# An attention and feed-forward kernel on one core: the second batch in split fp32r units in place of whole float32 pairs of heads

## The chip, the cores and the metric

The kernel runs on one core of a Trainium2 chip. The metric is the device time of one execution in microseconds. Unless a number is said to be of the profiled execution, times are medians of several executions. TensorE is called PE in the profile, its weight load PEld, VectorE is DVE, ScalarE is ACT, GpSimd is POOL, SyncE is SP.

## What is computed

Eight batches of eight heads, 576 positions and 64 dimensions go through attention with a sliding window of 128 positions and a linear bias per head; its output, 4608 tokens of 512 numbers, goes through a feed-forward layer with 2048 hidden units.

```
scores = scale * np.matmul(q, k.transpose(0, 1, 3, 2))
bias = slopes[:, None, None] * (-np.abs(rel).astype(np.float32))[None, :, :]
mask = (rel >= 0) & (rel < window)
scores = np.where(mask, scores + bias[None], -1000000000.0)
scores = scores - np.max(scores, axis=-1, keepdims=True)
attn = np.exp(scores)
attn = attn / (np.sum(attn, axis=-1, keepdims=True) + 1e-09)
attn_out = np.matmul(attn, v)
...
x = attn_out.transpose(0, 2, 1, 3).reshape(B * S, H * D)
h = x @ w_in
g = h * (1.0 / (1.0 + np.exp(-1.702 * h)))
out = g @ w_out
```

## The kernel before

**The feed-forward layer.** The tokens are cut into 18 chunks of 256, the hidden units into 16 groups of 128. One step is one chunk and one group: `up` makes h with twelve 128x256 matmuls (L552), ACT takes the tanh (L557), DVE makes g (L558), ACT casts it to fp32r as gh (L561), POOL makes the remainder gl = g - gh (L562), and `down` adds six 128x512 matmuls to the chunk's accumulators (L571): four with gh, two with gl. g, gh, gl and h have two buffers each. There are 288 steps. They go by chunk, but chunk 0 is done in two halves around chunk 1: steps 0 to 7 are chunk 0, steps 8 to 23 chunk 1, steps 24 to 31 the rest of chunk 0, and each later chunk has 16 steps. `split_x` makes high and low parts of a chunk of x (L536 on DVE or ACT, L538 on DVE and POOL).

**The weights** come as 64-bit words and are decoded once, in 32 halves: ACT L211, DVE L212 and L213, ACT L216, POOL L217. Three halves are decoded ahead of the steps and the rest in the first 22 or so steps.

**The attention of a batch** is made in one of two forms, chosen by the batch's number: below `WB` the whole form, from `WB` on the split form.

- *Whole form* (`part_batch`, `WholeUnit`): a unit is a pair of heads and a part of the positions (0 to 256, 256 to 512, 512 to 576), so 12 units to a batch. Everything stays float32. Scores are float32 matmuls of 64 rows of each head (L324, two records to a matmul in the trace), DVE adds the bias and takes the minimum (L351), ACT takes the exponential (L374), DVE the reciprocal (L392, L393). The normalization is done on POOL (L402) and ACT (L399) in turn, the transposes on PE (L419), ACT copies them out (L427), PE multiplies with v (L476), ACT copies the result to x (L485).
- *Split form* (`whole_batch`, `Unit`): both heads of a pair are laid end to end, 9 blocks of 128 positions, worked on by two (the last unit has one), so 5 units to a pair and 20 to a batch. Every operand is split in two fp32r numbers. ACT casts Q (L292) and V (L299), DVE casts K (L310), POOL makes the remainders of Q (L311), K (L312) and V (L300). Scores are two fp32r matmuls to a block (L334), then DVE L362, ACT L381, DVE L392 and L393, the normalization on DVE (L406), transposes (L442), ACT's cast of the transposed weights (L455), DVE's remainder (L461), the products with V (L499), and a sum of both halves: ACT L520, POOL L523, DVE L526 and L529. POOL clears parts of a block (L361, L367).

**What sets the order.** One `tick` moves all units in flight by one stage. The loop over the steps issues ticks at a pace that has each batch's units done before the chunk that reads them begins; the list `due` holds how many units are wanted and by which chunk. A unit of batch b may start when chunk `start` has begun. In the whole form each part of a batch has an entry of its own, by the chunk of its first position; in the split form the batch has one entry, by the chunk of its first position. A scheduler then moves instructions within each engine's queue, and each engine runs its queue in order. SP issues the loads, in program order; the loads of a unit are issued one tick after another, between the fetches of weights.

```
for b in range(B):
    start = max((b * S + S - 1) // T - XBUFS, 0)
    if b < WB:
        for lo, hi in ((0, 2 * P), (2 * P, 4 * P), (4 * P, S)):
            units += part_batch(b, lo, hi)
            due.append((len(units), (b * S + lo) // T, start))
    else:
        units += whole_batch(b)
        due.append((len(units), b * S // T, start))
```

Of the kernel before, what the change touches and what calls it, by code (L numbers as in the profile page):

```python
# [33 lines left out]
FAR = 1.0e37  # L34
DEPTH = 3
BESIDE = range(4)
WB = 2
DECODE_TICKS = 5, 6, 7
FETCH_AHEAD = 6
PINNED = 8  # L40
# [102 lines left out]
def tile_kernel(ctx: ExitStack, tc: tile.TileContext, q0, k0, v0, qT, kT, v, w_in, w_out, out):  # L143
# [9 lines left out]
    def move(dst, src):  # L153

        tc.keep_in_program_order(nc.sync.dma_start(dst, src))
# [78 lines left out]
    def load(u):  # L234
# [8 lines left out]
        u.rk = raw.tile([P, 3 * P], F32, name="rk", tag="rk")  # L243
        move(u.rq[:, :u.nq], qT[u.pair - WB * NP, :, u.q0:u.q0 + u.nq])
        move(u.rk[:, :u.nk], kT[u.pair - WB * NP, :, u.k0:u.k0 + u.nk])

# [24 lines left out]
    def load_v(u):  # L271
# [8 lines left out]
        if full:  # L280
            move(u.rv[:, :full], v[u.pair - WB * NP, at:at + full * P, :].rearrange("(c p) d -> p c d", p=P))
            u.spans.append((P, slice(0, full)))
        if full < len(u.loaded):
            m = u.loaded[-1].n
            move(u.rv[:m, full], v[u.pair - WB * NP, at + full * P:at + full * P + m, :])
            u.spans.append((m, slice(full, full + 1)))
# [306 lines left out]
# [4 lines that stand above are left out]
# [135 lines left out]
def lay_out(q, k, v, moe_w_in, moe_w_out):  # L732
    import numpy as np

    def pairs(a):

        n = len(a) * NP
        return np.asarray(a).reshape(n, 2, S, D).transpose(0, 1, 3, 2).reshape(n, P, S)
# [7 lines left out]
    def words(w):  # L746
# [5 lines left out]
    lay = {  # L752
        "q0": pairs(q[:WB]),
        "k0": pairs(k[:WB]),
# [19 lines left out]
```

## Time and profile before

| | us |
|---|---|
| median of 3 runs | 1064.5 |
| lowest and highest | 1063.76, 1065.91 |
| the profiled execution | 1068.36 |
| its span, from the first to the last instruction | 1066.3 |
| mean granted PE clock in the span | 0.995 of full speed |

The profile is of one execution. A line of a view names the kernel's line, the engine, the operation, what it writes and reads, the shapes and the count; then come the busy time in us and the mean ns of one, and the engine's idle time before it with what ended most of it. A line of a window gives its length and the busy time and count of instructions of PE, PEld, DVE, ACT and POOL, then the granted PE clock, the mean share in which the DMA engines were busy, and GB/s. A line of the timeline starts with the start and the duration in us. In the chain of work that ended last, each share is of the window asked for.

### The profile page before, as it was taken

The page shows a single profiled execution, that of the slowest core. Times are in us where ns is not written, and L with a number is a line of the kernel's source. Part 1 is how long each engine was busy: PE and PEld are TensorE (multiplying, and loading weights), DVE is VectorE, ACT ScalarE, POOL GpSimd, SP SyncE. Part 2 cuts the span into 40 slices and gives each one's busy share as a digit, 9 for nine tenths or more (in the row PEclk, how much of TensorE's full clock was granted, in tenths as well). Part 3 has the DMA queues.
Part 4 walks back from the last instruction along what each step waited for, and adds up shares of the span by engine and source line. Part 5 has one row for each costly group of instructions (what it writes and reads, how often), then busy time and mean ns, then how long its engine had stood idle before and what let it go on. Part 6 is the DMA issues. An engine that isn't in the chain of part 4 may idle for free.

```text
span 1066.3 us, 21362 instructions
## 1 busy us (share of the span) xinstructions
PE 1052.9 (99%) x7041; PEld 929.1 (87%) x7041; DVE 660.5 (62%) x2117; ACT 597.2 (56%) x1811; POOL 603.5 (57%) x863
## 2 busy tenths in 40 slices
PE   9899999999999999999999999999999999999998
PEld 5567787889989999999999999999999999998987
DVE  6797522568887777545767668767877687313121
ACT  6879853466666565535555556655665656322222
POOL 4579933567676666554656557656666665323232
PEclk9899999999999999999999999999999999999999
DMA  8872001223222132102121223212222221000000
GB/s 307 281 261 73 25 22 56 73 67 96 75 76 81 51 102 67 57 14 71 54 79 52 71 62 91 66 60 78 79 63 85 57 78 28 20 2 20 1 21 20
DMA packets 88109, 78.45 MB, mean 74 GB/s; under 512 B 36800, under 2 KB 79296, under 8 KB 88000
## 3 DMA queue, kind: packets, MB, share of 16 engines
q1 hardware_dynamic: 82240, 67.14, 21.4%
q10 hardware_dynamic: 5760, 9.96, 2.6%
q8 instruction: 55, 0.90, 0.3%
q14 instruction: 54, 0.44, 0.1%
HBM read 67.63 MB, written 9.44 MB: 72 GB/s over the span
## 4 chain that ended last, share of the span: by engine, by line
PE 94%; DVE 3%; ACT 1%; DMA 1%; issue 1%; POOL 0%; SPq 0%; DVEq 0%; POOLq 0%; ACTq 0%
PE h_ps L552 38%; PE acc L571 37%; PE s_ps L334 5%; PE x_ps L499 5%; PE t_ps L442 4%; PE x_ps L476 2%; PE t_ps L419 1%; PE sb_ps L324 1%; PE s_ps L324 1%; DVE wc L213 1%; DMA rw<-w_out 1%; ACT pb L374 1%; DVE rec L392 0%; PE acc L189 0%; DVE rw L212 0%
## 5 line engine op out<-in xcount | busy, mean ns | idle before, releaser
L562 POOL TENSOR_TENSOR gl<-g,gh 128x256 fp32r<-128x256 f32 x288 | 218.0, 757 | 292.2 <-ACT gh L561 224.9
L552 PE MATMUL h_ps<-xh,w 128*128 128x256 f32 x2304 | 370.2, 284 | 1.1 <-POOL w L217 0.6
L552 PEld LDWEIGHTS h_ps<-xh,w 128*128 128x128 f32 x2304 | 328.5, 189 | 34.5 <-issue 2.8
L571 PE MATMUL acc<-w,gh 128*128 128x512 f32 x1152 | 324.9, 400 | 0.0
L558 DVE SCALAR_TENSOR_TENSOR g<-g,h_ps 128x256 f32<-128x256 f32 x288 | 119.6, 415 | 207.9 <-ACT g L557 206.5
L557 ACT ACTIVATE g<-h_ps 128x256 f32<-128x256 f32 x288 | 110.4, 383 | 229.4 <-PE h_ps L552 207.3
L571 PEld LDWEIGHTS acc<-w,gh 128*128 128x128 f32 x1152 | 196.5, 189 | 27.9 <-ACT g L557 0.3
L552 PE MATMUL h_ps<-xl,w 128*128 128x256 f32 x1152 | 194.6, 280 | 0.0
L561 ACT CAST gh<-g 128x256 fp32r<-128x256 f32 x288 | 116.9, 406 | 129.5 <-DVE g L558 121.1
L571 PE MATMUL acc<-w,gl 128*128 128x512 f32 x576 | 188.0, 401 | 0.0
L552 PEld LDWEIGHTS h_ps<-xl,w 128*128 128x128 f32 x1152 | 164.2, 188 | 6.0
L312 POOL TENSOR_TENSOR K<-rk,K 128x384 fp32r<-128x384 f32 (+1 forms) x120 | 109.0, 909 | 65.2 <-ACT Q L292 15.9
L381 ACT ACTIVATE pb<-pb,mins 128x256 f32<-128x256 f32 (+2 forms) x216 | 104.9, 487 | 43.8 <-DVE mins L362 40.1
L571 PEld LDWEIGHTS acc<-w,gl 128*128 128x128 f32 x576 | 92.6, 188 | 9.5 <-issue 0.9
L311 POOL TENSOR_TENSOR Q<-rq,Q 64x256 fp32r<-64x256 f32 (+1 forms) x120 | 83.1, 692 | 22.2 <-DVE K L310 4.9
L406 DVE TENSOR_SCALAR pb<-pb,rec 128x256 f32<-128x256 f32 (+2 forms) x216 | 91.8, 461 | 3.2
L362 DVE CUSTOM_DVE_ANT_0 pb<-s_ps,bias 128x256 f32<-128x256 f32 (+3 forms) x240 | 85.7, 377 | 4.1 <-PE s_ps L334 2.8
L392 DVE TENSOR_SCALAR rec<-sums 128x2 f32<-128x2 f32 (+3 forms) x144 | 48.5, 336 | 58.4 <-ACT pb L381 53.6
L334 PE MATMUL s_ps<-K,Q 128*128 128x256 f32 (+1 forms) x432 | 79.8, 289 | 0.4 <-DVE mins L362 0.4
L310 DVE CAST K<-rk 128x384 fp32r<-128x384 f32 (+1 forms) x120 | 52.5, 438 | 41.2 <-PE s_ps L334 34.2
L461 DVE TENSOR_TENSOR pl<-t_ps,ph 128x512 fp32r<-128x512 f32 (+2 forms) x120 | 72.2, 604 | 9.3 <-ACT ph L455 6.6
L442 PE MATMUL t_ps<-ident,pb 128*128 128x128 f32 x408 | 74.2, 272 | 0.0
(68 smaller groups left out, 1322.2 us busy)
## 6 DMA issues: line engine op xcount, KB each, us to landing
rk<-kT SPq DMA_DIRECT2D x72, 192.0 KB, 2.5
rq<-qT SPq DMA_DIRECT2D x96, 128.0 KB, 2.3
out<-o ACTq DMA_DIRECT2D x36, 256.0 KB, 2.1
rw<-w_in SPq DMA_DIRECT2D x16, 512.0 KB, 6.5
rw<-w_out SPq DMA_DIRECT2D x16, 512.0 KB, 7.0
rk<-kT SPq DMA_DIRECT2D x48, 128.0 KB, 2.2
rv<-v SPq DMA_DIRECT2D x96, 64.0 KB, 1.9
rq<-q SPq DMA_DIRECT2D x16, 128.0 KB, 2.6
```

The lines of the kernel that those rows point to most:

```text
L312: nc.gpsimd.tensor_tensor(K2, rk, K1.bitcast(F32), ALU.subtract)
L334: nc.tensor.matmul(u.s[:b.rows, e, b.first:b.end], u.Q[:, b.q0 - u.q0:b.q0 - u.q0 + b.rows], k[:, ko:ko + b.end - b.first], start=(z == 0) ...
L362: nc.vector.tensor_tensor_reduce(b.p[ra:rb, cs:b.end], u.s[ra:rb, e, cs:b.end], bias[head][ra:rb, cs:b.end], -SCALE, BIG, ALU.add, ALU.min ...
L381: nc.scalar.activation(live, live, AF.Exp, bias=u.mins[:b.rows, e:e + 1], scale=-1.0, accum_out=u.sums[:b.rows, e:e + 1],)
L406: nc.vector.tensor_scalar(live, live, u.rec[:rows, e:e + 1], None, ALU.mult)
L442: nc.tensor.transpose(u.t[:c.n, w:w + b.rows], b.p[:b.rows, col:col + c.n], ident[:b.rows, :b.rows])
L552: nc.tensor.matmul(h, w1[f][:, z, k * P:(k + 1) * P], x[:, k], start=(n == 0), stop=(n == len(ops) - 1))
L557: nc.scalar.activation(g, h, AF.Tanh, scale=0.851)
L558: nc.vector.scalar_tensor_tensor(g, g, 1.0, h, ALU.add, ALU.mult)
L561: nc.scalar.copy(gh, g)
L562: nc.gpsimd.tensor_tensor(gl, g, gh.bitcast(F32), ALU.subtract)
L571: nc.tensor.matmul(acc, g[:, t * P:(t + 1) * P], w2[f][:, z], start=(f == self.f0 and n == 0), stop=(f == self.f1 - 1 and n == 2))
```

## The change

`WB` becomes 1. Batch 1 is then worked on in 20 split units in place of 12 whole ones. Batch 0 stays whole, batches 2 to 7 stay split. The arrays handed to the kernel are cut at the same place (`lay_out` uses `WB`).

```
-WB = 2
+WB = 1
```

In `due`, batch 1 had three entries, four units each, wanted by chunks 2, 3 and 4; now it has one, 20 units, wanted by chunk 2, that is by step 32. So the pace of units is higher up to step 32 and lower from there on.

On POOL, near the end of chunk 1, the order of before has these rows. The rows with gl are the 17th to 20th, the 21st to 23rd and the 24th to 26th; pb is a whole unit's weights, x_306 and xh are chunk 0's x for its second half.

```order
L562 TENSOR_TENSOR gl<-g,gh 128x256 x4
L402 TENSOR_SCALAR pb<-pb,rec 128x256 x2
L562 TENSOR_TENSOR gl<-g,gh 128x256 x3
L402 TENSOR_SCALAR pb<-pb,rec 64x192
L538 TENSOR_TENSOR xl<-x_306,xh 128x256 x2
L562 TENSOR_TENSOR gl<-g,gh 128x256 x3
```

In the changed kernel POOL has these rows ahead of the 22nd and 23rd gl, behind the 21st; K, Q and VV are the operands of split units of batch 1, xb and carry their sums, and w_15 the last two halves of weights.

```order
L312 TENSOR_TENSOR K_2294<-rk,K_2293 128x256
L311 TENSOR_TENSOR Q<-rq,Q 64x256
L300 TENSOR_TENSOR VV<-rv,VV 128x2x64
L523 TENSOR_TENSOR xb<-xb,carry 64x128
L300 TENSOR_TENSOR VV<-rv,VV 128x2x64
L311 TENSOR_TENSOR Q<-rq,Q 64x256
L312 TENSOR_TENSOR K_2369<-rk,K_2368 128x384
L217 TENSOR_TENSOR w_15_2189<-wc,w_15_2189 128x512
L217 TENSOR_TENSOR w_15_2271<-wc,w_15_2271 128x512
L300 TENSOR_TENSOR VV<-rv,VV 128x2x64
L312 TENSOR_TENSOR K_2440<-rk,K_2439 128x384
L562 TENSOR_TENSOR gl<-g,gh 128x256 x2
```

Nothing stood between the 21st and the 22nd gl before; now eleven operations do, and the last weights are decoded behind the 21st gl instead of ahead of the 17th.

On PE, the down products of the last but one step of chunk 1 (weights w_14) stood like this before, t_ps being a whole unit's transposes and acc_1195 and acc_1196 the chunk's accumulators:

```order
L571 MATMUL acc_1195<-w_14_1649,gh 128x512
L571 MATMUL acc_1196<-w_14_1649,gh 128x512
L419 MATMUL t_ps<-ident,pb 128x128
L571 MATMUL acc_1195<-w_14_1649,gl 128x512
L571 MATMUL acc_1196<-w_14_1649,gl 128x512
L419 MATMUL t_ps<-ident,pb 128x128 x5
L552 MATMUL h_ps<-xh,w_8_1013 128x256
```

and now like this, with the transposes and scores of a split unit behind them:

```order
L571 MATMUL acc_1347<-w_14_2106,gh 128x512
L571 MATMUL acc_1348<-w_14_2106,gh 128x512
L552 MATMUL h_ps<-xh,w_8_1013 128x256 x6
L571 MATMUL acc_1347<-w_14_2106,gl 128x512
L571 MATMUL acc_1348<-w_14_2106,gl 128x512
L442 MATMUL t_ps<-ident,pb 128x128 x2
L334 MATMUL s_ps<-K_2439,Q 128x256
```

The up products of two steps further on (w_8) have moved ahead of the products with gl, and split matmuls stand where whole ones stood.

## The prediction

> **What bounds the kernel now.** I read the page first, then stretches of the first 160 us, then the chain of work that ended last, each time asking which engine is last.
>
> ```profile
> PE 1052.9 (99%) x7041; PEld 929.1 (87%) x7041; DVE 660.5 (62%) x2117; ACT 597.2 (56%) x1811; POOL 603.5 (57%) x863
> by line: PE h_ps L552 37.7%; PE acc L571 37.3%; PE s_ps L334 4.7%; PE x_ps L499 4.6%; PE t_ps L442 4.2%; PE x_ps L476 2.0%; PE t_ps L419 1.2%; PE sb_ps L324 1.2%; PE s_ps L324 1.0%; DVE wc L213 0.8%; DMA rw<-w_out 0.7%; ACT pb L374 0.5%; is
> ```
>
> By the averages TensorE (PE) is the bound and every other engine has 40% to spare. So a change is worth what it takes off PE, wherever PE is last. But averages hide stages; these are three stretches (columns: us, then busy time of PE, PEld, DVE, ACT, POOL):
>
> ```profile
> 53.50:95.70 42.20, 39.27 (x253) 28.39 (x251) 38.37 (x86) 36.48 (x115) 35.25 (x33) 0.96 0.55 185
> 95.70:125.50 29.80, 29.80 (x190) 23.08 (x190) 17.19 (x55) 29.25 (x87) 27.24 (x25) 1.00 0.18 49
> 125.50:158.30 32.80, 32.80 (x200) 25.56 (x198) 10.61 (x30) 17.92 (x52) 17.10 (x20) 1.00 0.09 24
> ```
>
> Up to 125 us, while weights are still decoded, POOL is busy 84% and 91%, ACT 86% and 98%. Only from 125 us has everything but PE room. The change works in exactly these stretches.
>
> **What it saves on PE.** The chain's line above prices attention on PE: the split form (L334, L499, L442) holds 4.7 + 4.6 + 4.2 = 13.5% of 1066.3 us for six batches, so 24.0 us a batch, 0.113 us for each of 1,272 rows. The whole form is best read where PE alone is last, from the end of the 24th step's down products on:
>
> ```profile
> 161.24 0.63 PE L571 MATMUL acc<-w,gl 128*128 128x512 f32 x2
> by line: PE h_ps L552 41.1%; PE acc L571 37.9%; PE x_ps L476 10.8%; PE t_ps L419 3.4%; PE s_ps L334 2.7%; PE sb_ps L324 2.5%; PE s_ps L324 1.7%; PE t_ps L442 0.7%
> 1000.24 1.40 PE h_ps L552 x12
> ```
>
> The second row is the chain from 161.9 to 218 us: the last whole rows (L476, L419, L324) hold 18.4% of 56.1 us = 10.3 us. By the order, 28, 16 and 5 of them stand behind the 144th down product, the end of the 24th step. In the changed kernel none does; instead 2 more L334, 11 more L442 and 18 more L499 stand there, 31 x 0.113 = 3.5 us, and 22 fewer up products (1.40 / 12 = 0.117 us each, 2.6 us), which PE has done earlier. **PE's work behind the 24th step shrinks by 10.3 - 3.5 + 2.6 = 9.4 us.** Batch 2 is also no longer hurried beside the rest of batch 1. The DVE waits on the chain near 307 us may go with that: between 0 and 3.5 us, of which I take 1.1 (PE itself was hardly idle there). Together 10.5 us.
>
> **What it costs ahead of the 24th step.** POOL's rows by shape (mean ns behind the busy time):
>
> ```profile
> L562 POOL TENSOR_TENSOR gl<-g,gh 128x256 fp32r<-128x256 f32 x288 | 218.0, 757 | 292.2 <-ACT gh L561 224.9 <-issue 15.3 <-PE acc L571 14.6
> L312 POOL TENSOR_TENSOR K<-rk,K 128x384 fp32r<-128x384 f32 x72 | 73.4, 1020 | 42.8 <-ACT Q L292 8.9 <-PE x_ps L499 8.3 <-DVE K L310 6.0
> L311 POOL TENSOR_TENSOR Q<-rq,Q 64x256 fp32r<-64x256 f32 x96 | 71.5, 745 | 17.7 <-DVE g L558 4.5 <-DVE K L310 2.4 <-ACT Q L292 1.7
> L300 POOL TENSOR_TENSOR VV<-rv,VV 128x128 fp32r<-128x128 f32 x96 | 46.6, 486 | 10.7 <-ACT VV L299 7.1 <-DVE K L310 1.7 <-POOL Q L311 0.5
> L217 POOL TENSOR_TENSOR w<-wc,w 128x512 fp32r<-128x512 f32 x32 | 45.9, 1442 | 6.6 <-ACT w L216 6.4
> L312 POOL TENSOR_TENSOR K<-rk,K 128x256 fp32r<-128x256 f32 x48 | 35.6, 742 | 22.4 <-ACT Q L292 7.0 <-ACT g L557 3.6 <-PE s_ps L334 3.3
> L402 POOL TENSOR_SCALAR pb<-pb,rec 128x256 f32<-128x256 f32 x20 | 19.4, 980 | 13.0 <-DVE rec L393 9.5 <-ACT w L216 3.5
> L523 POOL TENSOR_TENSOR xb<-xb,carry 64x128 f32<-64x128 f32 x48 | 22.3, 465 | 8.9 <-ACT xb L520 7.6 <-PE s_ps L334 0.5
> L311 POOL TENSOR_TENSOR Q<-rq,Q 64x128 fp32r<-64x128 f32 x24 | 11.6, 482 | 4.5 <-DVE K L310 2.5 <-DVE pb L406 0.4
> L402 POOL TENSOR_SCALAR pb<-pb,rec 128x128 f32<-128x128 f32 x12 | 9.8, 821 | 11.4 <-DVE rec L393 11.4
> L300 POOL TENSOR_TENSOR VV<-rv,VV 128x64 fp32r<-128x64 f32 x24 | 8.4, 350 | 4.2 <-ACT VV L299 3.1
> L402 POOL TENSOR_SCALAR pb<-pb,rec 64x192 f32<-64x192 f32 x8 | 7.2, 895 | 1.6 <-DVE rec L393 1.6
> L538 POOL TENSOR_TENSOR xl<-xf,xh 128x256 fp32r<-128x256 f32 x34 | 28.1, 841 | 5.7 <-PE h_ps L552 3.2 <-DVE xh L536 1.7 <-PE acc L571 0.5
> L361 POOL MEMSET pb<- 64x192 f32 x24 | 6.9, 286 | 7.3 <-PE t_ps L442 4.6 <-PE t_ps L419 1.8
> L367 POOL MEMSET pb<- 128x64 f32 x24 | 3.7, 154 | 2.5 <-PE t_ps L442 2.4
> ```
>
> Count what stands in POOL's order between the 2nd gl (L562) and the 24th, both kernels; the orders part only behind the 3rd. Common to both: 22 gl, 27 weight halves (L217), 4 remainders of x (L538), 38.9, 16.7 and 3.4 us, and 4 normalizations of 64x192. Gone: 17 normalizations (L402), 12 x 0.980 + 4 x 0.821 + 0.895 = 15.9 us. New: K2, 12 x 1.020 + 8 x 0.742 = 18.2; Q, 16 x 0.745 + 4 x 0.482 = 13.8; VV, 13 x 0.486 + 3 x 0.350 = 7.4; five carry adds 2.3; four memsets of each kind 1.8. That is 43.5 us, **net +27.6 us: 78.4 us of POOL work become 106.0 us**, in a stretch that lasts 104.8 us, from the 2nd gl's end to the 24th's:
>
> ```profile
> 52.80 0.72 POOL L562 TENSOR_TENSOR gl<-g,gh 128x256 fp32r<-128x256 f32 x1
> 124.80 0.75 POOL L562 TENSOR_TENSOR gl<-g,gh 128x256 fp32r<-128x256 f32 x1
> 157.59 0.73 POOL L562 TENSOR_TENSOR gl<-g,gh 128x256 fp32r<-128x256 f32 x1 [1.13 <-ACT gh L561]
> ```
>
> (158.3 - 53.5.) PE's down product needs gl, at most two steps later (g, gh and gl have two buffers), so POOL's queue now paces PE. At which rate does POOL get through such a queue? Up to 95.7 us, the 8th gl, the order of before holds 13 L217, 6 gl, 10 L402 and 2 L538, 34.0 us of mean durations in 42.2 us, a rate r of 0.80; from there to the 15th gl (124.80 + 0.75, second row) 11 L217, 7 gl and 6 L402, 26.9 us in 29.8, r = 0.90; both 0.845. What is lost is idle time (waits for ACT and DVE) and operations longer than their mean. A reason for the second stands in the trace:
>
> ```profile
> 242.43 0.17 DVE L392 TENSOR_SCALAR rec<-sums 128x2 f32<-128x2 f32 x1 [0.79 <-ACT pb L381]
> 247.05 0.73 POOL L311 TENSOR_TENSOR Q<-rq,Q 64x256 fp32r<-64x256 f32 x1
> 247.18 0.63 DVE L392 TENSOR_SCALAR rec<-sums 128x2 f32<-128x2 f32 x1 [0.82 <-ACT pb L381]
> L406 DVE TENSOR_SCALAR pb<-pb,rec x216: 279/354/1626, 199.1 to 906.5; 128x256 f32<-128x256 f32 x84, 128x128 f32<-128x128 f32 x12, 128x192 f32<-128x192 f32 x12
> ```
>
> The same DVE instruction takes 0.17 us, or 0.63 when a POOL operation runs: it ends 0.03 us behind POOL's end (247.78). L406, SBUF to SBUF like it, spreads from 279 to 1626 ns about a median of 354 (last row). I take it that L310, a third of that kind, and L406 meet the same, and that POOL waits in turn for one that has started. Ahead of the 24th g the change adds 19 L310, 29 L406 and 7 L392 to DVE, so r will hardly rise above what it was. The Trainium skill says, in "SBUF — State Buffer", section "SBUF: two separate sides", that DVE in such modes and GpSimd share one pair of ports as an exclusive lock held for the whole instruction; the rows agree that one waits, but only 0.03 of the waiter's 0.17 us was left when POOL ended, so less than a whole instruction is exclusive.
>
> I take r = 0.845 up to the 15th gl, where 67.3 us of work now stand (79.6 us), and 0.90 behind it, where decoding thins out, for 38.7 us (43.0): **122.6 us instead of 104.8, +17.8** (r = 0.864 overall). Nothing less than 106.0 us (r = 1) is possible; r = 0.80 gives 132.5.
>
> One thing comes back. Where POOL is last PE follows its gl closely, where PE is last it lags:
>
> ```profile
> 83.26 1.18 POOL L562 TENSOR_TENSOR gl<-g,gh 128x256 fp32r<-128x256 f32 x1
> 84.74 0.64 PE L571 MATMUL acc<-w,gl 128*128 128x512 f32 x2
> ```
>
> 85.38 - 84.44 = 0.9 us here, against 161.87 - 158.32 = 3.6 us at the 24th: 2.5 us less.
>
> **Sum:** span change = 106.0 / r - 104.8 - 2.5 - 10.5 = 106.0 / r - 117.8. With 0.864 it is **+4.8 us**; I round to +4.5. The profiled execution would be 1068.4 + 4.5 = 1072.9 us (span 1066.3 + 4.5, and 2.1 around it); it lies 3.9 us above the runs' median of 1064.5, so the **forecast for the median is 1069.0 us**. The whole saving on PE is larger than 10.5 us, but what falls ahead of the 24th step is spent waiting for POOL.
>
> Costed at nothing, by these rows (busy us over six batches; then over two):
>
> ```profile
> L455 ACT CAST ph<-t_ps 128x512 fp32r<-128x512 f32 (+2 forms) x120 | 62.2, 519 | 5.3 <-PE t_ps L442 3.8 <-PE x_ps L499 0.7
> L292 ACT CAST Q<-rq 128x256 fp32r<-128x256 f32 (+1 forms) x120 | 46.2, 385 | 16.9 <-PE s_ps L334 12.7 <-DMA rq<-qT 1.9 <-DVE pb L406 0.6
> L520 ACT COPY xb<-x_ps 64x512 f32<-64x512 f32 (+1 forms) x72 | 39.5, 549 | 3.5 <-PE x_ps L499 1.8
> L299 ACT CAST VV<-rv 128x128 fp32r<-128x128 f32 (+1 forms) x120 | 34.3, 286 | 3.9 <-PE x_ps L499 2.2 <-DMA rv<-v 1.6
> L427 ACT COPY pw<-t_ps 128x512 f32<-128x512 f32 (+3 forms) x60 | 19.5, 365 | 2.4 <-PE t_ps L419 2.4
> L399 ACT ACTIVATE pb<-pb,rec 128x256 f32<-128x256 f32 (+2 forms) x36 | 16.3, 490 | 2.9 <-DVE rec L393 2.9
> ```
>
> ACT gains 182.2 / 6 = 30.4 us for a batch and loses 9.8 + 8.2, so at most 12.4 us come to the 83.7 us (36.48 + 29.25 + 17.92) that it works in the 104.8, and 122.6 hold them; the exponentials stay, 36 for 40. The new DMAs too: SyncE's queue gets rq, rk and rv loads of batch 1 ahead of the last weight pair, but DMA was busy 0.18 and 0.09 in the last two stretches. If that cover is gone, the last weight half comes late and r falls; that is inside the range.
>
> **Rivals.**
> - *PE stays the bound.* With the split work spread evenly POOL need not wait for whole units, and r rises above 0.90; then PE's saving shows. r = 0.965 gives -8.0 us (1056.5), r = 1 gives -11.8 (1053). For it: POOL 91% busy from 95.7 us with PE never idle. Against: r is a net rate over all waits, and the added DVE operations lengthen POOL's. It decides from r = 0.900, where the change is zero. Chance 0.27, of which 0.21 beyond -2.1 us.
> - *DVE and POOL hold each other up.* DVE was busy 38.37 of 42.2 us where r was 0.80. If that holds to the 24th step: 132.5 - 117.8 = +14.7 us, 1079. Against: from 95.7 us DVE had 42% to spare. Chance 0.26.
> - *Whole instructions exclude each other.* Then POOL also stands still for each of the 55 added DVE operations, at L406's median of 0.354 us some 20 us: near 1085. The quoted L392 speaks against it. Chance 0.05. (It is what the rule of the Trainium skill, "SBUF — State Buffer", would give, taken to the letter.)
> - That the change does nothing is excluded by the order.
>
> **Numbers.** The forecast (r 0.84 to 0.90, 1064.5 to 1073) has 0.42, of which 0.30 lie above +2.1 us. About 0.2%, 2.1 us, is what a measurement of this kernel can tell from no change. Slower: 0.30 + 0.26 + 0.05 = 0.61; faster 0.21; same 0.18. The range runs from r = 0.965 to r = 0.80, 1056 to 1080; it leaves out the end of the first rival (some 0.07) and the third with the tail of the second (0.11).
>
> **What would show it.** Right: in the changed profile the 24th gl ends near 176 us (158.3 + 17.8), POOL is busy over 85% from 53 to 170 us, PE has waits on POOL there, and from the 24th step's end to the end of the span takes some 10 us less than the 904.4 us (1066.3 - 161.9) of before. L392, L406 and L310 last longer between 60 and 170 us than later. Wrong: the 24th gl ends before 170 us with PE never waiting (first rival), or DVE is over 95% busy and later than POOL (second).

## The result, and the profile after

| | before | after |
|---|---|---|
| median, us | 1064.17 (1063.76 to 1065.91, 4 runs) | 1076.58 (1075.88 to 1077.26, 4 runs) |
| ratio to before, 95% interval | | 1.0113 [1.0096, 1.0131] |
| profiled span, us | 1066.3 | 1074.6 |
| from the 2nd gl's end to the 24th's | 104.8 | 129.4 |
| from the 24th step's end to the end of the span | 904.4 | 892.2 |

The changed kernel is 12.4 us slower. The spans differ by only 8.3 us because the profiled execution of before had begun late: its 2nd gl ended at 53.5 us, that of after at 49.8. So the table goes by stretches. Medians in this document are over all executions of a run and ratios over the fast ones alone; two executions were far slower than the rest, one of e4_no_k2 (2998.53 us) and one of order3_e7 (1097.36 us).

The page of after, its first row: busy time and share of each engine. PE has 10.2 us less to do than before (1052.9), and yet the span is longer.

```profile
PE 1042.7 (97%) x6989; PEld 936.4 (87%) x6989; DVE 717.7 (67%) x2245; ACT 600.6 (56%) x1803; POOL 634.0 (59%) x919
```

The ends of the stretch in the timeline of after: the 2nd gl, the 24th gl, and the last down products of the 24th step (start and duration in us).

```profile
49.09 0.73 POOL L562 TENSOR_TENSOR gl<-g,gh 128x256 fp32r<-128x256 f32 x1
178.52 0.73 POOL L562 TENSOR_TENSOR gl<-g,gh 128x256 fp32r<-128x256 f32 x1
181.81 0.62 PE L571 MATMUL acc<-w,gl 128*128 128x512 f32 x2
```

49.8 to 179.25 is 129.4 us, and PE ends its 24th step at 182.4, 3.2 us behind the gl (before: 3.6).

The windows of that stretch, first before, then after, whole (us, then busy us of PE, PEld, DVE, ACT, POOL, then the granted PE clock, DMA share, GB/s):

```profile
53.50:158.30 104.80, 101.86 (x640) 77.03 (x638) 66.17 (x167) 83.65 (x251) 79.59 (x75) 0.98 0.30 96
```

```profile
49.80:179.30 129.50, 108.10 (x660) 91.78 (x659) 117.52 (x281) 91.12 (x264) 109.09 (x127) 0.91 0.35 107
```

and after by thirds, the ends being the 8th and 15th gl, as the prediction cut them:

```profile
49.80:96.70 46.90, 36.97 (x216) 28.76 (x216) 43.60 (x83) 31.22 (x96) 40.58 (x40) 0.85 0.58 192
96.70:132.70 36.00, 28.00 (x165) 24.85 (x165) 30.57 (x80) 24.77 (x68) 29.42 (x36) 0.91 0.16 45
132.70:179.30 46.60, 43.12 (x282) 38.17 (x280) 43.34 (x120) 35.13 (x101) 39.08 (x52) 0.96 0.26 68
```

DVE is the row to see. It was busy 63% of this stretch before and is busy 91% after, 93%, 85% and 93% in the thirds. POOL is busy 84%, ACT 70%, PE 83%. The groups of DVE's instructions in the stretch, before and after (count, busy us, mean ns, idle time ahead):

```profile
L213 DVE SCALAR_TENSOR_TENSOR wc<-wc,rw 128x512 int32<-128x512 int32 x26 | 28.3, 1094 | 9.4 <-ACT wc L211 9.4
L392 DVE TENSOR_SCALAR rec<-sums 128x4 f32<-128x4 f32 (+1 forms) x12 | 7.7, 638 | 1.0 <-ACT pb L374 1.0
```

```profile
L213 DVE SCALAR_TENSOR_TENSOR wc<-wc,rw 128x512 int32<-128x512 int32 x26 | 26.3, 1018 | 0.5 <-ACT wc L211 0.4
L406 DVE TENSOR_SCALAR pb<-pb,rec 128x256 f32<-128x256 f32 (+2 forms) x31 | 23.1, 783 | 0.5
L310 DVE CAST K<-rk 128x384 fp32r<-128x384 f32 (+1 forms) x20 | 14.2, 708 | 2.1 <-issue 0.7 <-PE s_ps L334 0.7 <-POOL w L217 0.6
L392 DVE TENSOR_SCALAR rec<-sums 128x2 f32<-128x2 f32 (+2 forms) x21 | 11.2, 532 | 1.6 <-ACT pb L381 1.3
L461 DVE TENSOR_TENSOR pl<-t_ps,ph 128x512 fp32r<-128x512 f32 (+2 forms) x15 | 9.0, 603 | 2.5 <-ACT ph L455 2.5
L529 DVE TENSOR_TENSOR xf<-x_ps,xb 64x192 f32<-64x192 f32 (+3 forms) x19 | 5.3, 310 | 0.1
```

Their spread over the whole of after (shortest, median and longest, in ns):

```profile
L213 DVE SCALAR_TENSOR_TENSOR wc<-wc,rw x32: 664/694/2516, 19.9 to 163.9; 128x512 int32<-128x512 int32 x32
L392 DVE TENSOR_SCALAR rec<-sums x152: 131/170/2936, 7.9 to 914.4; 128x2 f32<-128x2 f32 x112, 128x1 f32<-128x1 f32 x28, 128x4 f32<-128x4 f32 x8, 64x2 f32<-64x2 f32 x4
L393 DVE RECIPROCAL rec<-rec x152: 141/165/178, 8.1 to 914.5; 128x2 f32<-128x2 f32 x112, 128x1 f32<-128x1 f32 x28, 128x4 f32<-128x4 f32 x8, 64x2 f32<-64x2 f32 x4
L310 DVE CAST K<-rk x140: 276/354/2100, 62.1 to 901.9; 128x384 fp32r<-128x384 f32 x84, 128x256 fp32r<-128x256 f32 x56
L406 DVE TENSOR_SCALAR pb<-pb,rec x252: 278/354/2555, 76.2 to 915.1; 128x256 f32<-128x256 f32 x98, 128x128 f32<-128x128 f32 x14, 128x192 f32<-128x192 f32 x14
```

Four of these lines take far longer in the stretch than their median: L406 31 x (783 - 354) = 13.3 us, L310 20 x (708 - 354) = 7.1, L392 21 x (532 - 170) = 7.6, L213 26 x (1018 - 694) = 8.4. That is an estimate of 36 us of waiting inside DVE's instructions; the two lines of before give 26 x (1094 - 694) + 12 x (638 - 170) = 16 us. So by this estimate, of DVE's additional 51 us some 20 are waiting and 31 are work. L393 reads and writes SBUF too, and never takes over 178 ns.

That the long instructions wait for POOL, and for what, can be read from their ends. Five rows of one place of after:

```profile
108.86 1.48 POOL L312 TENSOR_TENSOR K<-rk,K 128x384 fp32r<-128x384 f32 x1
109.57 0.80 DVE L392 TENSOR_SCALAR rec<-sums 128x2 f32<-128x2 f32 x1
111.23 1.43 POOL L217 TENSOR_TENSOR w<-wc,w 128x512 fp32r<-128x512 f32 x1
111.42 1.46 DVE L310 CAST K<-rk 128x384 fp32r<-128x384 f32 x1
112.62 0.84 POOL L562 TENSOR_TENSOR gl<-g,gh 128x256 fp32r<-128x256 f32 x1
```

L392 ends 0.03 us behind the end of POOL's L312, and L310 0.22 us behind that of L217. Taken over the stretch, and calling an instruction long when it takes over 1.25 times the median of its form: all 8 long L392 of 128x2 end 23 to 26 ns behind the end of a POOL operation, all 8 long L310 of 128x384 212 to 219 ns, 16 of 17 long L406 of 128x256 146 to 153 ns, and 14 of 15 long L213 545 to 555 ns. POOL waits as well: the gl in the last row ends 0.58 us behind L310, and each of the 11 gl of the stretch that take over 770 ns ends 584 to 603 ns behind the end of an L212, L213, L310 or L406. But POOL loses less by it. Against the medians of their forms its operations of the stretch are some 10 us longer, an estimate like the 36 us of DVE.

Who waits for whom, in the waits of after from 40 to 185 us (us in total, times, longest):

```profile
ACT gh L561 <- DVE g L558: 12.4, 12, 1.9
PE h_ps L552 <- DVE g L558: 9.2, 7, 3.1
ACT w L216 <- DVE wc L213: 7.3, 12, 1.8
PE acc L571 <- POOL gl L562: 1.6, 1, 1.6
```

and the chain of work that ended last in the same window, behind that of before from 40 to 165 us:

```profile
by line: PE h_ps L552 27.1%; PE acc L571 23.6%; PE x_ps L476 9.6%; PE t_ps L419 6.9%; DVE wc L213 6.9%; PE sb_ps L324 5.6%; PE s_ps L324 5.1%; DVE rec L392 3.3%; DVE rw L212 3.0%; DVE pb L351 2.4%; issue 2.3%; POOL w L217 1.1%; POOL pb L402
```

```profile
by line: DVE wc L213 11.1%; DVE pb L406 9.7%; PE h_ps L552 9.0%; PE acc L571 8.2%; DVE rec L392 6.6%; issue 5.8%; DVE K L310 5.7%; DVE pb L362 5.1%; DVE rw L212 4.5%; ACT pb L381 3.9%; DMA rw<-w_out 3.6%; DVE g L558 3.0%; PE t_ps L442 2.5%;
```

PE waits for DVE's g (9.2 us), not for POOL's gl (1.6); ACT waits for DVE as well; and on the chain DVE's seven lines hold 45.7%, PE's three 19.7%, and POOL has none among those listed. Before, the six lines of PE that are listed held 77.9% and the four of DVE 15.6%.

### The profile page after: what moved, and what is told of

Its sections match the earlier page's. It is cut to its first block, busy times and chain, and to the rows that moved or that the text cites. A ratio compares the mean times of both kernels' runs of the same rounds, so it can differ in the third digit from the quotient of the medians.

```text
span 1074.6 us, 21533 instructions
## 1 busy us (share of the span) xinstructions
PE 1042.7 (97%) x6989; PEld 936.4 (87%) x6989; DVE 717.7 (67%) x2245; ACT 600.6 (56%) x1803; POOL 634.0 (59%) x919
## 4 chain that ended last, share of the span: by engine, by line
PE 87%; DVE 8%; ACT 2%; DMA 2%; issue 1%; SPq 0%; POOL 0%; DVEq 0%; POOLq 0%; ACTq 0%
PE acc L571 35%; PE h_ps L552 35%; PE x_ps L499 5%; PE s_ps L334 5%; PE t_ps L442 5%; DVE wc L213 1%; DVE pb L406 1%; DMA rw<-w_out 1%; DVE rec L392 1%; DVE K L310 1%; DVE pb L362 1%; DVE rw L212 1%; ACT pb L374 1%; ACT pb L381 1%; PE acc L189 0%
## 5 line engine op out<-in xcount | busy, mean ns | idle before, releaser
L312 POOL TENSOR_TENSOR K<-rk,K 128x384 fp32r<-128x384 f32 (+1 forms) x140 | 130.0, 929 | 77.8 <-ACT Q L292 12.7
L381 ACT ACTIVATE pb<-pb,mins 128x256 f32<-128x256 f32 (+2 forms) x252 | 122.4, 487 | 51.5 <-DVE mins L362 47.6
L406 DVE TENSOR_SCALAR pb<-pb,rec 128x256 f32<-128x256 f32 (+2 forms) x252 | 116.4, 499 | 3.6
L311 POOL TENSOR_TENSOR Q<-rq,Q 64x256 fp32r<-64x256 f32 (+1 forms) x140 | 98.9, 707 | 23.2 <-DVE g L558 4.4
L362 DVE CUSTOM_DVE_ANT_0 pb<-s_ps,bias 128x128 f32<-128x128 f32 (+1 forms) x280 | 99.9, 376 | 5.2 <-PE s_ps L334 3.9
L334 PE MATMUL s_ps<-K,Q 128*128 128x256 f32 (+1 forms) x504 | 93.7, 291 | 0.2
L392 DVE TENSOR_SCALAR rec<-sums 128x2 f32<-128x2 f32 (+3 forms) x152 | 53.8, 354 | 59.0 <-ACT pb L381 55.4
L461 DVE TENSOR_TENSOR pl<-t_ps,ph 128x512 fp32r<-128x512 f32 (+2 forms) x140 | 84.0, 603 | 10.8 <-ACT ph L455 8.2
L310 DVE CAST K<-rk 128x384 fp32r<-128x384 f32 (+1 forms) x140 | 64.6, 461 | 37.1 <-PE s_ps L334 34.7
L442 PE MATMUL t_ps<-ident,pb 128*128 128x128 f32 x476 | 87.6, 277 | 1.2 <-DVE pb L406 1.1
```

The source lines that it names most:

```text
L312: nc.gpsimd.tensor_tensor(K2, rk, K1.bitcast(F32), ALU.subtract)
L334: nc.tensor.matmul(u.s[:b.rows, e, b.first:b.end], u.Q[:, b.q0 - u.q0:b.q0 - u.q0 + b.rows], k[:, ko:ko + b.end - b.first], start=(z == 0) ...
L362: nc.vector.tensor_tensor_reduce(b.p[ra:rb, cs:b.end], u.s[ra:rb, e, cs:b.end], bias[head][ra:rb, cs:b.end], -SCALE, BIG, ALU.add, ALU.min ...
L381: nc.scalar.activation(live, live, AF.Exp, bias=u.mins[:b.rows, e:e + 1], scale=-1.0, accum_out=u.sums[:b.rows, e:e + 1],)
L406: nc.vector.tensor_scalar(live, live, u.rec[:rows, e:e + 1], None, ALU.mult)
L442: nc.tensor.transpose(u.t[:c.n, w:w + b.rows], b.p[:b.rows, col:col + c.n], ident[:b.rows, :b.rows])
```

## The experiments

Four theories stood at the start. **Theory 1:** DVE's operations from SBUF to SBUF and POOL's operations wait for each other, and DVE, full with work and waits, is last up to the 24th gl. **Theory 2:** the amount of POOL's work makes the loss, as the prediction had it. **Theory 3:** the amount of DVE's work makes it, without mutual waits. **Theory 4:** the earlier date (chunk 2 for all of batch 1), not the form. Shares are busy shares in the stretch from the 2nd to the 24th gl; "rest" is from the 24th step's end on.

| run | median us | ratio to before, 95% | stretch | rest | DVE | POOL |
|---|---|---|---|---|---|---|
| e1_pace | 1063.91 | 0.9999 [0.9988, 1.0010] | 112.4 | 895.2 | 61% | 73% |
| e2_one_port | 1068.53 | 1.0041 [1.0026, 1.0056] | 115.8 | 896.8 | 90% | 90% |
| e3_k_act | 1069.90 | 1.0046 [1.0029, 1.0063] | 123.7 | 893.0 | 88% | 85% |
| e4_no_k2 | 1064.55 | 1.0003 [0.9993, 1.0012] | 118.0 | 893.9 | 92% | 76% |
| e5_no_eps | 1075.23 | 1.0086 [1.0063, 1.0109] | 124.7 | 893.8 | 92% | 88% |
| e6_no_eps_one_port | 1064.64 | 0.9993 [0.9982, 1.0004] | 113.7 | 894.0 | 91% | 93% |
| e7_no_eps_one_port_k_act | 1061.99 | 0.9974 [0.9960, 0.9987] | 117.1 | 891.3 | 86% | 93% |
| one_port_k_act | 1062.92 | 0.9980 [0.9964, 0.9995] | 117.2 | 893.6 | 84% | 91% |
| e8_before_no_eps | 1074.24 | 1.0076 [1.0059, 1.0093] | 105.9 | 909.9 | 58% | 70% |
| order2_before | 1071.29 | 1.0065 [1.0050, 1.0080] | 113.0 | 907.1 | 61% | 73% |
| order2_after | 1081.70 | 1.0165 [1.0133, 1.0198] | 129.5 | 896.8 | 92% | 85% |
| order2_one_port | 1074.57 | 1.0082 [1.0056, 1.0108] | 122.4 | 896.0 | 90% | 90% |
| order3_before | 1067.59 | 1.0030 [1.0020, 1.0040] | 104.8 | 905.9 | 64% | 76% |
| order3_after | 1078.09 | 1.0131 [1.0116, 1.0147] | 133.1 | 896.0 | 89% | 79% |
| order3_one_port | 1068.29 | 1.0033 [1.0018, 1.0048] | 122.3 | 892.9 | 90% | 87% |
| order3_e7 | 1072.07 | 1.0051 [1.0031, 1.0071] | 121.3 | 891.8 | 83% | 89% |

**The date without the form** (e1_pace). The edit, on the kernel before:

```
-            due.append((len(units), (b * S + lo) // T, start))
+            due.append((len(units), (b * S + (0 if b else lo)) // T, start))
```

> The kernel before, with batch 1 still in whole pairs, but all three of its parts wanted by chunk 2, as the split units are. It keeps the form and takes the changed pace. If the pace makes the loss (units crowded ahead of step 32), the stretch from the 2nd to the 24th gl grows from 104.8 by 20 us or more and the time is near 1075. If the form makes it, only PE's whole rows (10.3 us, now behind the 24th step) move ahead of it: the stretch is 112 to 117 us, the rest falls from 904.4 to about 894, and the time stays at 1062 to 1067.

```profile
49.50:161.90 112.40, 109.69 (x686) 80.21 (x686) 68.71 (x181) 89.22 (x275) 81.81 (x79) 0.98 0.33 105
```

PE is busy 109.69 of 112.40 us; the stretch is 7.6 us longer, the rest 9.2 shorter, and the time is that of before within 0.12%, as expected if the form makes the loss. Theory 4 falls: the early date moves PE's work and costs nothing by itself.

**The normalization in another form** (e2_one_port). The edit, on the changed kernel:

```
-            nc.vector.tensor_scalar(live, live, u.rec[:rows, e:e + 1], None, ALU.mult)
+            if u.pair // NP == 1:
+                nc.vector.tensor_scalar(live, live, u.rec[:rows, e:e + 1], None, ALU.mult, ALU.add,
+                                        accum_out=u.mins[:rows, 2 + e:3 + e])
+            else:
+                nc.vector.tensor_scalar(live, live, u.rec[:rows, e:e + 1], None, ALU.mult)
```

`u.pair // NP` is the batch.

> The changed kernel, with batch 1's normalization on DVE (L406) given an accumulator that nobody reads. By itself the operation should get longer, by about 0.1 us. Theory 1 (DVE's operations from SBUF to SBUF wait for POOL's and the other way round, and DVE is last ahead of the 24th gl): if the form with an accumulator doesn't wait for POOL, the 31 of them in the stretch fall from 783 to about 500 ns, 8.8 us of DVE's time, and the time from 1076.6 to 1069 to 1073. Theory 2 (the amount of POOL's work alone): 1076.6 within 1. Theory 3 (the amount of DVE's work alone, no mutual waits): 31 x 0.1 us slower, 1078 to 1080.

The spread of that line in this run, the operation and its second record, which reads the accumulator out:

```profile
L407 DVE TENSOR_SCALAR_CACHE_REDUCE pb<-pb,rec x36: 333/475/483, 77.3 to 182.6; 128x256 f32<-128x256 f32 x28, 128x128 f32<-128x128 f32 x4, 128x192 f32<-128x192 f32 x4
L407 DVE DVE_READ_ACCUMULATOR pb<-pb,rec x36: 74/82/84, 77.6 to 183.0; 128x1 f32 x36
```

And its stretch:

```profile
50.90:166.70 115.80, 100.58 (x633) 85.06 (x632) 104.21 (x289) 87.03 (x253) 104.39 (x119) 0.93 0.36 112
```

The operation now takes 333 to 483 ns, though all 29 of them in the stretch ran beside a POOL operation, and 82 more for the accumulator. So it is longer than the plain form's median (475 + 82 against 354), and never longer than that; the plain form went up to 2555. The time falls by 8.0 us. Theory 3 has it the wrong way round (slower) and theory 2 at no change; theory 1 stands, its range of 1069 to 1073 missed by half a microsecond. The whole stretch moved more than the 8.8 us of L406 (13.6 us). The order differs between the kernels (29 of these operations stand in its stretch, 31 stood there), and the rest gave 4.6 us back.

**K's cast on ACT** (e3_k_act).

```
-        nc.vector.tensor_copy(K1, rk)
+        (nc.scalar.copy if u.pair // NP == 1 else nc.vector.tensor_copy)(K1, rk)
```

> The changed kernel, with batch 1's cast of K (L310) on ACT instead of DVE: 20 operations of 708 ns, 14.2 us, leave DVE in the stretch to the 24th gl, and ACT, busy 91.1 of 129.5 us, gets about 20 x 0.45 = 9 us. POOL's work stays. Theory 1: the stretch falls by 8 to 13 us and the time to 1064 to 1069. Theory 2 (POOL's amount alone): 1076.6 within 1.5. Theory 3 (DVE's amount alone, at the durations without POOL, 20 x 0.3 us): 1070 to 1072.

```profile
48.90:172.60 123.70, 103.54 (x657) 86.25 (x655) 109.28 (x257) 95.64 (x281) 105.74 (x126) 0.96 0.36 109
```

6.7 us less: theory 2 falls again, but 1069.9 lies between the ranges of theories 1 and 3 and doesn't part them.

**POOL without the remainder of K** (e4_no_k2), the remainder left out for batch 1, whose second score matmul reads the high part `u.K1` in its place (the lines for that are not shown):

```
-        nc.gpsimd.tensor_tensor(K2, rk, K1.bitcast(F32), ALU.subtract)
+        if u.pair // NP != 1:
+            nc.gpsimd.tensor_tensor(K2, rk, K1.bitcast(F32), ALU.subtract)
```

> The changed kernel, without batch 1's remainder of K (POOL, L312): the second score matmul of batch 1 takes K's high part again, so its scores are other numbers, and PE has as many rows as before. 20.9 us of busy POOL time leave the stretch, DVE's instructions stay. Theory 2 (POOL's amount alone): 18.2 us of work at r = 0.82, so the stretch is 22 us shorter and the time near 1055. Theory 1: DVE is relieved too, since it waits for fewer POOL operations, but only by what it waited for these, 20 x 0.35 to 0.6 us: 7 to 12 us, 1065 to 1070. Theory 3 (DVE's amount alone): 1076.6 within 1.5.

```profile
51.30:169.30 118.00, 103.38 (x647) 88.40 (x647) 108.30 (x271) 89.04 (x261) 89.21 (x106) 0.91 0.37 113
```

With 20 us less to do POOL is busy only 76%, yet the stretch is 11.4 us shorter, not 22, and DVE is still busy 92% of it. Its own busy time fell from 117.52 to 108.30 us with nearly the same instructions. Theory 2's 1055 is excluded, and so is theory 3's no change: work taken off POOL shortens DVE's instructions. 1064.55 is just below theory 1's range.

**The addition of 1e-9 left out** (e5_no_eps, and e8_before_no_eps on the kernel before).

```
-        nc.vector.tensor_scalar(u.rec[:rows, :ne], u.sums[:rows, :ne], 1e-9, None, ALU.add)
-        nc.vector.reciprocal(u.rec[:rows, :ne], u.rec[:rows, :ne])
+        if u.whole or u.pair // NP < 2:
+            nc.vector.reciprocal(u.rec[:rows, :ne], u.sums[:rows, :ne])
+        else:
+            nc.vector.tensor_scalar(u.rec[:rows, :ne], u.sums[:rows, :ne], 1e-9, None, ALU.add)
+            nc.vector.reciprocal(u.rec[:rows, :ne], u.rec[:rows, :ne])
```

> The changed kernel; for batches 0 and 1 the reciprocal (L393) reads the sums directly, so the addition of 1e-9 on DVE (L392) is left out (a row's sum is at least 1, since its largest term is exp(0), so the addition changes nothing in float32). 21 operations of 532 ns, 11.2 us, leave DVE ahead of the 24th gl; by themselves they take about 0.165 us, 3.5 us together. The reciprocal never lasts over 0.178 us in the traces, whatever POOL does. Theory 1 (mutual waits, DVE last): a part of the wait falls to the next operation, so 4 to 11 us faster, 1066 to 1073. Theory 2 (POOL's amount): 1076.6 within 1. Theory 3 (DVE's amount alone): 1073.

> The kernel before the change, without the addition of 1e-9 in batches 0 and 1. If DVE and its waits for POOL bound the stretch of 53.5 to 95.7 us already (DVE 38.37 of 42.2 us busy), 12 operations of 638 ns leave it and the time falls by 3 to 6 us, to 1058 to 1061. If DVE was last in the changed kernel alone, it stays at 1064 within 1.

Both missed. e5 gained 1.4 us by the medians, with an interval that leaves room for none: it lies outside all three ranges, nearest to theory 2's, and by itself speaks against theory 1. L212, the shift of the weights' low words, in the stretch of after, and in that of e5:

```profile
L212 DVE TENSOR_SCALAR rw<-rw 128x512 int32<-128x512 int32 x15 | 8.9, 599 | 0.0
```

```profile
L212 DVE TENSOR_SCALAR rw<-rw 128x512 int32<-128x512 int32 x14 | 15.7, 1124 | 0.0
```

Its 14 operations took 15.7 us where 15 had taken 8.9: 6.8 us, beside the 11.2 that L392 had held. In after the longest L392 starts at 58.5 us and takes 2936 ns; in e5 an L212 starts at 57.5 us and takes 3470. The likely reading is that an operation that waits can't be priced by its duration, since what it waits for is still there when it is gone. It is not shown apart from the order: in order3_one_port, below, L212 takes 1154 ns on average with the addition in place. e8 was worse than either expectation, 9.5 us slower than the runs of before beside it; its stretch is 1.1 us longer and its rest 5.5. An instruction less on DVE can't lengthen the rest by itself; what else differs is the order, in all queues. Why this order is a bad one stays open.

**Order alone.** That miss puts every run above in doubt, since each edit also moved the order. So the kernels before and after were made in two more orders, with the same instructions: the second calls `mix` ahead of `scores` in a tick, the third `split_rest` right behind `split_q`.

```
         stage(-2, high, low)
+        stage(-3, mix)
         stage(0, scores)
-        stage(-3, mix)
```

```
         stage(1, split_q)
+        stage(1, split_rest)
         stage(-2, flip, split_v)
...
-        stage(1, split_rest)
```

> The kernel before the change; in a tick, mix is called ahead of scores instead of behind it. The same instructions; the scheduler puts them in another order in all queues (for PE, DVE and POOL). Every edit so far has also moved the order, so this measures what order alone does. If order matters little: 1064 within 3. If it matters as much as the edits did: up to 10 us off.

> The changed kernel with the same exchange of mix and scores. If the loss of 12 us is the change's own (DVE full ahead of the 24th gl), it stands against the kernel before in this order too: 8 to 16 us longer than that, DVE over 90% busy from the 2nd to the 24th gl. If it was an unlucky order, the two come within 4 us of each other.

> The kernel before the change; in a tick, split_rest (the cast of K and the remainders) is called right behind split_q, ahead of flip. The same instructions in a third order. As with the second order: 1064 within 3 if order matters little.

> The changed kernel in the third order. The change's own loss: 8 to 16 us longer than the kernel before in that order. An unlucky order: within 4 us of it.

The stretches: second order before and after, third order before and after.

```profile
45.90:158.90 113.00, 106.92 (x650) 78.05 (x650) 69.09 (x176) 86.70 (x259) 82.29 (x76) 0.98 0.35 117
```

```profile
47.10:176.60 129.50, 108.55 (x662) 88.53 (x662) 119.66 (x278) 93.70 (x273) 110.19 (x125) 0.92 0.40 126
```

```profile
49.40:154.20 104.80, 100.46 (x641) 75.82 (x639) 67.08 (x167) 83.80 (x253) 79.51 (x75) 1.00 0.32 104
```

```profile
48.20:181.40 133.20, 112.75 (x651) 94.99 (x650) 118.00 (x271) 91.96 (x265) 105.56 (x122) 0.86 0.34 105
```

Order alone moves the kernel before by 7.0 and 3.3 us (ratios 1.0065 and 1.0030). But the change costs 10.4 us in the second order (1081.70 - 1071.29) and 10.5 in the third (1078.09 - 1067.59), beside 12.4 in its own, and each time DVE goes from some 60% to 90%. The loss is the change's own.

> The changed kernel in the second order with the accumulator at batch 1's normalization. If DVE's waits for POOL make the loss: 5 to 10 us less than the changed kernel in that order (1081.7), 1072 to 1077. If the gain in the first order was the order's luck: within 3 of 1081.7, on either side.

> The changed kernel in the third order with the accumulator at batch 1's normalization. DVE's waits: 5 to 10 us less than 1078.1, 1068 to 1073. Luck: within 3 of 1078.1.

The accumulator form saves 7.1 and 9.8 us in these orders, 8.0 in the first, and in none do the intervals of the two forms meet. That is theory 1, shown in three orders: the edit makes DVE's work longer and leaves POOL the same operations, and the time falls because some 30 operations no longer wait for POOL. The amount of DVE's work is the other half of theory 1: the cast of K taken off DVE was worth 6.7 us.

**More relief.** e6 has no addition and the accumulator; e7 has K's cast on ACT as well; one_port_k_act has the accumulator and the cast.

> The changed kernel with both: no addition of 1e-9 in batches 0 and 1, and the accumulator at batch 1's normalization. If the mutual waits are the cause and DVE is still last, the gains add up to a part: 1061 to 1066, the stretch near 108 us. PE's busy time of 1041 us and as much idle time as before (13.4) would give 1056 to 1057, which is the least. If the two relieve the same wait, it stays at 1068.

> The kernel before this one, with batch 1's cast of K (L310) on ACT as well: DVE loses another 12 us. If DVE is still last, 1056 to 1061. ACT was busy 96% of the stretch with that cast; if ACT is last by now, 1062 to 1068, and DVE's share falls below 85%.

> The changed kernel in the first order with the accumulator and with batch 1's cast of K on ACT, the addition of 1e-9 kept. Alone the two saved 8.0 and 6.7 us. If both are waits and work of one full engine, DVE, they add to most of that: 1062 to 1066. If another engine takes over (ACT), 1068 as with the accumulator alone.

> The changed kernel in the third order with all three edits (no addition of 1e-9 in batches 0 and 1, accumulator, cast of K on ACT). If the relief of DVE is what counts: 12 to 16 us less than 1078.1, so 1062 to 1066, and less than the kernel before in that order, 1067.6. If not: above 1068.

e6 came out in its range (1064.64), with a stretch of 113.7 us where 108 was expected. e7's stretch:

```profile
50.00:167.00 117.00, 103.23 (x657) 85.74 (x657) 100.80 (x286) 98.15 (x292) 108.64 (x128) 0.96 0.39 117
```

DVE is down to 86%, ACT is at 84%, and POOL at 93%. By these shares POOL is the fullest now, and not ACT, as e7's second case had it. That case rested on a slip: ACT's 95.64 us in e3 were read as 96%, but they are 77% of 123.70 us. PE's waits for DVE's g are 2.6 us in this stretch, where the changed kernel had 9.2. In the first order e7 (0.9974) and one_port_k_act (0.9980) are 2.7 and 1.6 us faster than the runs of before beside them, and their intervals leave 1 out; the two can't be told apart. In the third order the three edits missed their range of 1062 to 1066: 1072.07, with a wide spread (1067.39 to 1073.59, and the one of 1097.36), where the accumulator alone gave 1068.29 and the kernel before 1067.59. So a version faster than both kernels exists, by 0.26% [0.13, 0.40], but less than order alone moves; the relief of DVE undoes the loss, and whether it leaves a gain is a matter of the order.

## Why the prediction was right in sign and too small

**PE's saving behind the 24th step** was predicted as 9.4 us of work and 1.1 of waits, 10.5. Measured: 904.4 - 892.2 = 12.2. The mechanism was right, the place only in part. The windows up to the 40th step and from the 49th to the 64th, before and after:

```profile
161.90:222.50 60.60, 60.60 (x393) 49.25 (x392) 23.58 (x75) 26.82 (x96) 26.35 (x37) 1.00 0.23 67
253.80:316.00 62.20, 61.77 (x435) 56.91 (x434) 52.98 (x178) 40.96 (x127) 44.58 (x71) 1.00 0.30 85
```

```profile
182.40:239.10 56.70, 56.34 (x386) 51.24 (x385) 43.89 (x146) 35.76 (x112) 38.28 (x60) 1.00 0.31 89
270.30:325.80 55.50, 55.50 (x383) 51.06 (x382) 41.50 (x140) 33.19 (x101) 34.85 (x55) 1.00 0.26 73
```

3.9 us fall up to the 40th step (60.60 to 56.70), 6.7 from the 49th to the 64th (62.20 to 55.50), the others 1.6. The whole rows are gone from the first, but units of batch 2 have moved up into it; the second has 52 PE records fewer (435 to 383), and the waits for DVE there, 0.43 us of idle PE, are gone too.

**POOL's additional work** was predicted as 27.6 us; its busy time in the stretch rose by 29.5 (79.59 to 109.09). Right.

**The rate at which POOL gets through it is the step that failed**: "I take r = 0.845 up to the 15th gl, where 67.3 us of work now stand (79.6 us), and 0.90 behind it, where decoding thins out". Measured: 132.7 - 49.8 = 82.9 us up to the 15th gl, r = 67.3 / 82.9 = 0.812, and 46.6 us behind it, r = 38.7 / 46.6 = 0.830. Together 106.0 / 129.4 = 0.819 in place of 0.864, and the stretch grew by 24.6 us in place of 17.8. This is 6.8 of the 7.9 us that were missed. What stood behind it: 0.90 was read off POOL's queue in a stretch in which DVE had room (17.19 of 29.8 us busy), 0.845 is the mean of that stretch and of the one where DVE was nearly full (38.37 of 42.2 us, r = 0.80), and both were carried into a stretch that the change fills on DVE. POOL wasn't the engine that was last. From 53 to 170 us it was busy 84%, where the prediction's sign asked for over 85%; PE waited 1.6 us for POOL's gl and 9.2 for DVE's g.

**The lag** of PE behind gl was to shrink by 2.5 us, since PE would follow POOL. It went from 3.6 to 3.2. Another 2.1 us, for the same reason: PE follows DVE's g.

The sum with measured terms: 24.6 - 0.4 - 12.2 = +12.0 us, beside 12.4 by the medians.

**The rivals.** *DVE and POOL hold each other up* was the right one: r = 0.80 and 1079 us predicted, 0.819 and 1076.6 measured. What the prediction held against it, "from 95.7 us DVE had 42% to spare", is the mistake in one sentence: the change itself puts 31 L406, 20 L310, 15 L461 and 9 more L392 into that spare time. The prediction had counted the new operations by line, but took them only as a reason for POOL's rate not to rise, and never added them up as time on DVE. By the medians L406 and L310 are 31 x 0.354 + 20 x 0.354 = 18 us; with L461 (9.0) and L529 (5.3) 32 us, about the added work estimated above; 66.17 + 32 = 98 us of DVE before any wait is longer, and the waits then make 117.5 of it. Its sign, DVE over 95% busy, was set too high: 91% was enough. *PE stays the bound* didn't come about: PE idled 21.4 us of the stretch (129.50 - 108.10). *Whole instructions exclude each other* (near 1085) didn't either.

**L392, L406 and L310 longer ahead of the 24th step than later**: right, on average 556, 800 and 725 ns from 60 to 170 us, and 332, 462 and 423 behind that. ACT's work and the DMAs stayed covered, as costed: ACT was busy 91.12 of 129.5 us, and with batch 1's casts of K on ACT as well, 9.4 us (e3), the time fell.

## What to carry to other kernels

Where a change adds work to several engines in one stage, add up each engine's time in that stage, with durations as they are while the others work, and not as the median or the page's mean has them; an engine's idle time is what the added work is paid from, and no evidence that it stays idle. Between DVE and POOL a busy neighbour is part of the price: a form of the DVE operation that is longer by itself but never waits was worth 7 to 10 us here. And a gain of a few us is to be shown in more than one order of the queues before it is believed.

## What the runs showed of the hardware that was not expected

- Which DVE operations wait for POOL depends on the form, not only on where the data lie. The plain scaling from SBUF to SBUF lasted up to 2555 ns, the same scaling with an accumulator at most 483. The reciprocal, SBUF to SBUF with one input, never took over 178 ns, where the addition ahead of it took up to 2936. With the addition gone (e5) it took at most 179, so it is not the addition that waits in its place. The Trainium skill, in "VectorE: DVE Perf Modes", section "What auto-detection actually checks", gives the two-port mode to operations whose single source and destination lie in SBUF, with their outermost dimensions both even or equal, as far as firmware enables it for the operation. L406, L310 and L392 waited and meet that description; the reciprocal and the accumulating form meet it too and didn't wait, so by this page the difference would lie in what is enabled, which no run here shows. L213, which has two inputs in SBUF and which that sentence doesn't cover, waited as well, up to 2516 ns.
- What is left of a DVE operation when POOL's ends is nearly a constant of its form: 23 to 26 ns for L392 of 128x2, 146 to 153 for L406 of 128x256, 212 to 219 for L310 of 128x384. Each is less than the shortest time of that line in any shape in after (131, 278 and 276 ns), so a part of what the profile shows as the operation had passed beside POOL's.
- Waiting may pass on: without L392, L212 went from 599 to 1124 ns; order alone is not ruled out.
- The order of the queues alone, with the same instructions, is worth 3.3 and 7.0 us (0.3% and 0.65%).
- The granted PE clock in the stretch fell from 0.98 to 0.91 while PE idled more; it was 0.86 to 0.92 in the changed kernel's other orders. What that costs was not tried, but it doesn't go with the time: e4 had 0.91 as well and ran 12 us faster than the changed kernel.
